# Two row vectors spread by VectorE, half rows interleaved on TensorE, and a new order of steps in a fused linear-attention and feed-forward kernel

## The chip, the cores and the metric

The kernel runs on one core of a Trainium2 chip. The metric is the time of one execution on the device in microseconds, the median of the runs. The engines are TensorE (PE; its weight loads are listed as PEld), VectorE (DVE), ScalarE (ACT), GpSimd (POOL) and SyncE (SP), which here only issues DMAs. Each engine works through its own list in order, and they meet at semaphores.

## The reference

```python
batch, n_heads, seq, head_dim = (4, 8, 768, 48)      # r, k, v; w and u are (n_heads, head_dim)
for t in range(S):
    cur = np.einsum('bhd,bhe->bhde', u[None] * kt, vt)
    y[:, :, t] = np.einsum('bhd,bhde->bhe', rt, state + cur)
    state = w[None, :, :, None] * state + np.einsum('bhd,bhe->bhde', kt, vt)
...
x = attn_out.transpose(0, 2, 1, 3).reshape(B * S, H * D)   # 3072 x 384
h = np.maximum(x @ w_in, 0.0)                              # w_in 384 x 2048
return h * h @ w_out                                       # w_out 2048 x 384
```

## The kernel before

The sequence is cut into chunks of 128 positions. A unit is one chunk of one batch with all eight heads, so there are 24 units, in the order of `UNITS`. Within a chunk the recurrence is written as products with a mask; between chunks a state per batch is carried along. Units 0 to 3 (two pairs, chunks 0 and 1 of batches 0 and 1) are loaded pair by pair: a partition of such a load holds two neighbouring positions, rows 0 to 63 belong to the first chunk and rows 64 to 127 to the second.

The whole program is one list of steps, `ORDER`, written out by hand or by a planner: name, unit or group, engine (P, D, A, G, S) and buffers or PSUM banks. A loop at the end issues the steps; each engine gets its own in the order of the list, and what stands between them on other engines is ordered only by the data, the buffers and the eight banks. The steps:

- `w`, `u` load the two vectors, `lw` takes the logarithm of w, `bw` and `bu` spread log w and u over 128 partitions by a product with a row of ones, `Wk` and `Wt` are the powers of w for k and r (Exp with a scale per partition; 0 and 1 for the pairs, 2 for the rest), `bc`, `WLcol` and `WLm` make the factor of a whole chunk.
- `lp`, `ld` load r, k, v (pairs, single units); `V` and `W` load quarters of the two weight matrices as bf16, from GpSimd's queue.
- `kh`, `rh` scale k and r into the tile rk; `vb` casts v. `P0`, `P1`, `du`, `dv` make the term with u. `TK`, `TR` with `KC`, `RC` transpose k and r of a pair; `T` with `Tc` does it for a unit on TensorE, `XB` by a DMA transpose.
- `A` (`Ap` for pairs) are the products k r, `Bm` (`Bp`) puts the mask on them, `Y` sums what goes to y, `U` is k v for the state, `S0`, `ts`, `S` carry the state.
- `xs` copies y out of PSUM, `X` and `xTc` transpose it on TensorE, `xX` by a DMA transpose.
- `F1` is a part of the first layer for a group of one or two units (`GROUPS`), `re` the maximum with 0, `sq` the square, `F2` a quarter of the second layer for a unit, `Fh` the same for half of the columns, `os` and `oh` copy out of PSUM, `out` and `outh` write to memory.
- `Z` are products of the identity with itself that nobody reads.

In `Y` and `U`, a unit of a pair uses only its 64 rows of the operands, and the two units of a pair are two separate steps. F1 has four parts per group of one unit and eight per group of two; a part fills one bank, which `re` must empty before the next user.

## Time and profile before

| | us |
|---|---|
| median of 3 runs (lowest, highest) | 172.89 (172.86, 173.21) |
| span of the profiled execution | 170.9 |
| TensorE busy | 163.7 |
| VectorE busy | 135.7 |
| ScalarE busy | 101.8 |
| GpSimd busy | 98.6 |
| granted TensorE clock, mean | 1.000 |

The profile covers one execution from its first to its last instruction; that is the span, and no other time is given for that execution. The time of a run has some microseconds around the span (172.89 against 170.9). Busy times of TensorE overlap, since a product's end is modelled and the next begins before it; the chain that ended last gives the pace of products better. In the groups of instructions a row names the line, the engine, the operation and its output and input tiles.

### The profile page before, as it was taken

How to read it: one execution, taken by the hardware profiler on the slowest of the kernel's cores; microseconds unless marked ns; L12 is line 12 of the kernel's file. 1: busy time of each engine (PE TensorE's matmuls, PEld its weight loads, DVE VectorE, ACT ScalarE, POOL GpSimd, SP SyncE). 2: the span in 40 equal slices, each digit the busy share in tenths (PEclk: the TensorE clock that was granted, in tenths of full speed). 3: DMA queues.
4: the chain of work that ended last, by engine and by line, in shares of the span. 5: the costliest groups of instructions: out<-in, count | busy, mean ns of one | idle time of the engine just before them, and what ended most of it. 6: DMA issues, size and time to landing. Idle time of an engine off the chain costs nothing.

```text
span 170.9 us, 4599 instructions
## 1 busy us (share of the span) xinstructions
PE 163.7 (96%) x1828; PEld 125.3 (73%) x1828; DVE 135.7 (79%) x255; ACT 101.8 (60%) x190; POOL 98.6 (58%) x120
## 2 busy tenths in 40 slices
...
GB/s 143 322 233 193 220 175 197 211 201 74 185 197 192 165 185 230 200 161 227 162 118 184 227 167 251 200 65 115 208 97 207 162 85 69 70 118 0 6 138 92
DMA packets 96297, 27.56 MB, mean 161 GB/s; under 512 B 90514, under 2 KB 96276, under 8 KB 96276
## 3 DMA queue, kind: packets, MB, share of 16 engines
...
q0 software_dynamic: 2688, 3.15, 10.7%
...
q14 instruction: 7, 0.06, 0.1%
...
## 4 chain that ended last, share of the span: by engine, by line
PE 76%; DMA 7%; POOL 7%; ACT 3%; SPq 2%; issue 2%; ACTq 0%; POOLq 0%
PE bank L532 29%; PE bank L504 29%; DMA ldk<-in_k_dram 3%; PE bank L410 3%; DMA ldr<-in_r_dram 2%; DMA out_dram<-os 2%; POOL rk L336 2%; POOL P L342 2%; PE bank L363 2%; PE bank L462 2%; SPq L320 2%; PE bank L451 2%; PE bank L546 2%; PE bank L488 1%; PE bank L449 1%
## 5 line engine op out<-in xcount | busy, mean ns | idle before, releaser
L504 PE MATMUL bank<-xT,W 128*128 128x256 bf16 (+1 forms) x672 | 70.0, 257 | 1.3 <-ACT hr L514 0.8
L532 PE MATMUL bank<-W,hq 128*128 128x384 bf16 x368 | 68.9, 326 | 0.0
L504 PEld LDWEIGHTS <-W 128*128 128x128 bf16 x672 | 57.1, 98 | 9.1 <-issue 1.5
L514 ACT ACTIVATE hr<-bank 128x512 bf16<-128x512 f32 x67 | 38.5, 594 | 35.4 <-PE bank L504 24.0
L532 PEld LDWEIGHTS <-hq 128*128 128x128 bf16 x368 | 33.7, 98 | 18.1
L521 ACT ACTIVATE hq<-hr 128x512 bf16<-128x512 bf16 x70 | 41.0, 626 | 3.4 <-DVE hr L516 2.8
L418 DVE TENSOR_TENSOR Bm<-bank,maskJT 128x512 bf16<-128x512 f32 x40 | 25.7, 681 | 2.7 <-PE bank L410 2.7
L516 DVE TENSOR_SCALAR hr<-bank 128x512 bf16<-128x512 f32 x29 | 19.8, 686 | 7.8 <-PE bank L504 5.3
L354 POOL TENSOR_TENSOR dv<-ldv,du 128x384 f32<-128x384 f32 (+1 forms) x18 | 15.9, 894 | 15.4 <-DVE du L349 10.5
L346 POOL TENSOR_TENSOR P<-P,ub 128x384 f32<-128x384 f32 x15 | 16.0, 1072 | 13.7 <-DVE P L342 13.3
L339 POOL TENSOR_TENSOR rk<-ldr,Wt 128x384 bf16<-128x384 f32 x15 | 16.1, 1081 | 0.0
L523 DVE TENSOR_TENSOR hq<-hr 128x512 bf16<-128x512 bf16 x26 | 12.8, 506 | 3.2 <-ACT hr L514 3.0
L483 POOL TENSOR_TENSOR S0W<-ts,WLm 128x384 bf16<-128x384 f32 x10 | 10.8, 1076 | 6.5 <-DVE ts L480 5.7
L342 POOL TENSOR_TENSOR P<-ldr,ldk 128x384 f32<-128x384 f32 x13 | 13.3, 1022 | 1.2 <-DMA ldk<-in_k_dram 1.1
L474 DVE TENSOR_TENSOR xs<-bank,dv 128x384 bf16<-128x384 f32 x20 | 11.1, 553 | 3.0 <-PE bank L451 1.1
L336 POOL TENSOR_TENSOR rk<-ldk,Wk 128x384 bf16<-128x384 f32 x12 | 12.6, 1054 | 0.7 <-DMA ldk<-in_k_dram 0.7
L349 DVE TENSOR_REDUCE du<-P 128x8 f32<-128x384 f32 x24 | 12.8, 542 | 0.0
L252 DVE COPY os<-bank 128x384 f32<-128x384 f32 x11 | 6.1, 551 | 6.6 <-PE bank L532 6.6
L250 ACT COPY os<-bank 128x384 f32<-128x384 f32 (+1 forms) x14 | 6.3, 460 | 7.2 <-DMA out_dram<-os 2.6
L480 DVE TENSOR_TENSOR ts<-bank,S0W 128x384 f32<-128x384 f32 x16 | 8.7, 549 | 1.2 <-POOL S0W L483 0.8
L451 PE MATMUL bank<-vb,Bm 128*128 128x48 bf16 x160 | 9.5, 183 | 0.0
L451 PEld LDWEIGHTS <-Bm 128*128 128x128 bf16 x160 | 8.2, 96 | 1.0
...
## 6 DMA issues: line engine op xcount, KB each, us to landing
...
```

What stands on the lines that cost most here:

```text
L336: e.tensor_mul(rk[slot[f"rk{i}"]][:, 1, :, 0:D], loaded("k", i), Do.factor("k", i % 2 if i < PAIRED else 2))
L339: e.tensor_mul(rk[slot[f"rk{i}"]][:, 0, :, 0:D], loaded("r", i), Do.factor("t", i % 2 if i < PAIRED else 2))
L342: e.tensor_mul(P0b[slot[f"P{i}"]], loaded("r", i), loaded("k", i))
L346: e.tensor_mul(t, t, bank("bu")[:, 0 : H * D].rearrange("p (h d) -> p h d", h=H) if i in EARLY_U else ub)
L354: e.tensor_mul(dv_of(i) if i < PAIRED else dvb[slot[f"dv{i}"]], loaded("v", i), t)
L418: e.tensor_mul(Bmb[slot[f"Bm{i}{h}"]], heads(bank(f"bA{i}{h}"), 128), mask_b)
L451: e.matmul(y[:, hc, D * h : D * (h + 1)], m[h][:, hc, :], vb[:, 2 * hc + h, :], start=(c == 0), stop=True, skip_group_check=True,)
L504: e.matmul(hp[:, fi, :], W1[f // 4][:, c, 256 * (f // 2 % 2) : 256 * (f // 2 % 2 + 1)].rearrange("p (m j) -> p j m", j=2)[:, f % 2, :], xt ...
L514: e.activation(hr, hp, AF.Relu)
L516: e.tensor_scalar_max(hr, hp, 0.0)
L521: e.activation(hq, hr, AF.Square)
L532: e.matmul(bank(f"bO{i}")[:, 0:d_model], hqb[slot[f"hq{g},{f // m}"]][:, at : at + L], W2[q][:, f % 4, :], start=(seen[i] == 1 and f % 4 = ...
```

## The change

- `w` and `u` are loaded into four partitions (0, 32, 64, 96) of cleared tiles, and VectorE's stream shuffle copies each of those rows to the 32 partitions of its quarter (`wsh`, `ush`). `lw` runs on 128 partitions, `Wk` and `Wt` read its output from SBUF. `bw`, `bu` and the copy `ub` go. `w` stays on ScalarE's queue, `u` moves to SyncE's.
- The clearing of the tiles rk beyond the first four and of WLm moves to GpSimd (`mR`, `mW`).
- For the pairs, `Y` becomes `YD` (both units of a pair in one step, with the products on rows 0 to 63 and 64 to 127 alternating) and `YI` (the part with the state); `U` becomes `UP`, alternating in the same way.
- The empty products, 8 + 2 + 7 in three places, become 28 at the start of TensorE's list.
- All steps have a new order and partly another engine. Steps by engine, before and after: sq on ScalarE 70 and 51, on VectorE 26 and 45; os on ScalarE 12 and 20, on VectorE 11 and 3; re on VectorE 29 and 25; kh on VectorE 12 and 7; rh on VectorE 9 and 13; T 3 and 5, XB 17 and 15; X 16 and 10, xX 8 and 14.

Removed code of functions is not repeated here; it stands above.

```diff
-EARLY_U = ()
 ORDER = """
-w:A mP.0:G mP.1:G lp.r.0:S/0 lp.k.0:S/0 tab:A lw:A Z.8:P/0 bw:P/0 lp.r.1:S/1 lp.v.0:S/0 mJ:G u:A lp.k.1:S/1 Wt.1:A/1
-lp.v.1:S/1 bc:P/2 P0.1:G/0 Wk.0:A/3 rh.1:D/0 ld.r.5:S/4 Wt.0:A/4 bu:P/5 kh.0:D/1 V.3:G WLcol:A P0.0:D/1 Wk.1:A/6
-rh.0:D/1 TR.0:P/7 ld.k.4:S/4 V.0:G rh.3:D/2 ub:A V.1:G rh.2:D/3 vb.0:A/0 vb.1:A/1 ld.r.4:S/5 kh.1:D/0 P1.0:G RC.0:A/0
-TR.1:P/2 kh.2:D/3 kh.3:D/2 TK.0:P/1 KC.0:A/1 V.2:G P1.1:D U.1:P/5 Z.2:P/4 TK.1:P/4 ld.k.5:S/5 du.0:D/0 dv.0:G RC.1:A/2
-du.1:D/1 dv.1:G Ap.0.1:P/7/3 Bp.0.1.1:D/0 vb.3:A/2 U.0:P/6 Ap.0.0:P/1/2 Bp.0.1.0:D/1 Bp.0.0.1:D/2 WLm:G KC.1:A/3
-Z.7:P/3 Ap.1.0:P/3/7 vb.2:A/3 U.3:P/2 Bp.0.0.0:D/3 P0.2:G/2 U.2:P/4 S0.0:D Y.0:P/1 ld.v.4:S/4 S0.2:D P1.2:G Y.1:P/6
-xs.0:A/0 ts.3:D/0 ts.1:D/1 X.0:P/4 Ap.1.1:P/1/2 xTc.0:D/0 du.2:D/2 xs.1:A/1 X.1:P/5 F1.0.3:P/4 xTc.1:A/1 P0.3:G/3
-P1.3:G Bp.1.0.1:D/4 F1.0.0:P/6 re.0.3:D/0 dv.2:G F1.1.3:P/5 Wt.2:A re.0.0:A/1 W.1:G Bp.1.1.1:D/5 du.3:D/3 ld.v.5:S/5
-Bp.1.0.0:D/6 Wk.2:A F1.1.0:P/4 F1.1.1:P/6 dv.3:G re.1.0:A/2 F1.0.1:P/0 rh.5:G/4 re.1.3:A/3 Bp.1.1.0:D/7 Y.3:P/4
-sq.1.3:A/0 re.0.1:A/4 W.2:G kh.4:D/5 re.1.1:A/5 sq.1.0:D/1 Y.2:P/5 ld.k.6:S/6 xs.3:D/2 W.3:G F1.0.2:P/0 xs.2:A/3
-rh.4:D/5 sq.0.0:A/2 X.3:P/6 W.0:G X.2:P/4 re.0.2:D/3 F1.1.2:P/5 xTc.3:A/0 sq.0.3:A/3 xTc.2:D/0 re.1.2:A/2 P0.4:D/4
-T.4:P/0 Tc.4:D/4 F1.2.4:P/6 F1.2.7:P/4 sq.1.2:D/4 F1.2.5:P/5 re.2.4:D/1 re.2.7:A/0 ld.r.6:S/6 sq.0.2:A/5 F1.2.1:P/0
...
+Z.28:P/0 lp.r.0:S/0 u:S nj:D w:A wsh:D tab:A ush:D lw:A bc:P/1 mW:G Wt.0:A/2 lp.k.0:S/0 rh.0:D/0 Wt.1:A/3 rh.1:D/1
+TR.0:P/4 Wt.2:A Wk.1:A/5 lp.k.1:S/1 mP.0:G Wk.0:A/6 mP.1:G P0.1:D/0 kh.1:D/1 P1.1:D WLcol:A RC.0:A/0 kh.0:D/0 TK.0:P/7
+KC.0:A/1 kh.3:D/3 kh.2:D/2 TK.1:P/0 KC.1:A/2 lp.r.1:S/1 rh.2:D/2 du.1:D/0 mJ:G P0.0:G/1 P1.0:G du.0:D/1 rh.3:D/3
+lp.v.0:S/0 vb.0:A/0 Ap.0.0:P/1/5 Bp.0.0.0:D/0 Ap.0.1:P/6/4 vb.1:A/1 ld.r.5:S/4 Bp.0.1.1:D/1 Bp.0.0.1:D/2 TR.1:P/2
+V.2:G Bp.0.1.0:D/3 UP.0:P/7/3 WLm:G S0.0:D RC.1:A/3 Ap.1.1:P/0/1 lp.v.1:S/1 Ap.1.0:P/4/5 V.3:G vb.2:A/2 dv.0:G dv.1:G
+YD.0:P/2/6 YI.1:P Bp.1.0.1:D/4 V.0:G vb.3:A/3 UP.1:P/7/5 Bp.1.0.0:D/5 ts.1:D/0 xs.0:A/0 X.0:P/2 xTc.0:D/0 Bp.1.1.0:D/6
+xs.1:A/1 X.1:P/4 F1.0.2:P/6 P0.3:G/2 P1.3:G du.3:D/2 xTc.1:A/1 P0.2:G/3 P1.2:G F1.1.2:P/3 Wk.2:A F1.1.3:P/2 F1.0.3:P/4
+Bp.1.1.1:D/7 du.2:D/3 dv.2:D re.1.3:A/0 sq.1.3:A/0 S0.2:D dv.3:G YD.1:P/0/1 xs.2:A/2 YI.3:P xs.3:A/3 F1.1.0:P/2
+re.0.3:A/1 mR:G F1.0.0:P/7 X.2:P/0 re.0.2:D/2 ld.k.5:S/4 X.3:P/6 V.1:G re.1.0:A/3 ts.3:D/1 re.1.2:A/4 kh.5:G/4
+rh.5:D/4 T.5:P/5 sq.1.2:A/1 ld.r.4:S/5 ld.k.4:S/5 kh.4:D/5 rh.4:G/5 T.4:P/1 Tc.4:A/4 xTc.3:D/0 xTc.2:D/0 F1.2.0:P/4
+P0.4:D/4 F1.2.1:P/2 re.2.1:A/5 F1.2.5:P/6 P0.5:G/0 re.0.0:A/0 Tc.5:D/5 ld.v.5:S/4 ld.r.6:S/6 P1.5:G P1.4:G W.1:G
+du.5:D/4 sq.2.1:A/2 re.2.0:A/4 A.5:P/3/0 sq.0.3:D/3 vb.5:A/4 A.4:P/5/1 sq.1.0:A/4 F1.2.7:P/2 rh.6:G/6 re.2.5:A/1
+ld.k.6:S/6 kh.6:G/6 du.4:D/0 dv.5:D F1.2.6:P/7 Bm.4.1:D/0 F1.2.3:P/1 re.2.3:A/5 F1.0.1:P/4 sq.0.2:A/5 F1.1.1:P/6
+re.1.1:A/3 ld.v.4:S/5 sq.1.1:A/6 dv.4:G ld.k.10:S/7 U.5:P/1 Bm.4.0:D/1 Bm.5.0:D/2 Bm.5.1:D/3 Y.5:P/5 re.0.1:A/2
+ld.r.7:S/7 vb.4:D/5 Y.4:P/3 T.6:P/0 F1.2.2:P/6 xs.5:D/4 ld.k.9:S/1 X.5:P/5 xs.4:D/0 ld.k.7:S/0 ld.v.7:S/6 S0.5:D
+xTc.5:D/1 Tc.6:D/6 sq.2.3:D/7 re.2.6:D/3 S.3:G X.4:P/3 F1.2.4:P/4 xTc.4:A/1 U.4:P/1 S0.4:D ld.v.6:S/7 sq.2.5:D/8
...
+sq.3.4:A/18 ld.k.12:S/4 F1.3.7:P/6 re.3.7:A/4 F2.3.1:P/7 Y.6:P/0 Y.7:P/6 F2.2.3:P/1 F2.3.3:P/7 F2.2.0:P/1 os.2:A/0
+dv.7:G xs.7:D/1 ld.r.13:S/4 X.7:P/6 xTc.7:A/2 rh.9:D/2 xs.6:D/2 X.6:P/0 xTc.6:A/2 ts.6:D/0 ld.v.9:S/0 sq.3.5:D/19
+re.3.0:A/3 P0.9:D/3 XB.9:S/2 F2.0.0:P/3 sq.3.1:D/20 F2.5.2:P/5 F1.4.5:P/1 S.6:D rh.8:D/3 F2.1.3:P/2 os.3:A/1 rh.10:G/0
+F1.4.3:P/6 F1.4.7:P/0 re.4.3:A/0 P0.8:D/0 re.4.5:D/2 F1.4.2:P/4 ld.k.11:S/5 F1.4.0:P/7 A.9:P/1/6 sq.3.3:A/21 P1.9:D
+P1.8:G sq.4.3:D/22 re.4.2:D/1 sq.4.5:A/23 re.4.0:A/0 du.8:D/3 re.4.7:A/5 F2.1.0:P/2 os.1:A/2 sq.3.0:A/24 F1.4.6:P/4
+re.4.6:A/2 sq.4.6:A/25 vb.9:D/0 Bm.9.0:D/2 F1.4.4:P/7 F2.0.3:P/3 re.4.4:A/3 rh.13:D/4 Bm.9.1:D/3 kh.8:G/3 P0.10:G/4
+ld.r.11:S/5 P0.11:D/2 ld.k.13:S/0 P1.11:D ld.v.10:S/1 P1.10:D sq.3.7:A/26 os.0:A/3 F2.4.1:P/0 T.10:P/1 Tc.10:A/0
+sq.4.4:D/27 U.9:P/2 F2.5.1:P/5 F2.4.2:P/0 kh.13:G/4 kh.11:D/5 Y.9:P/6 P0.13:G/1 sq.4.7:D/9 A.10:P/4/7 du.9:D/4
+XB.8:S/3 dv.9:D xs.9:D/3 A.8:P/3/1 Bm.8.1:D/0 Bm.8.0:D/1 ld.v.8:S/3 du.10:D/0 ld.v.13:S/2 rh.12:D/1 vb.10:A/1
+sq.4.2:A/6 F2.4.3:P/0 rh.11:G/5 ld.v.11:S/4 XB.11:S/5 F1.4.1:P/6 out.2:S re.4.1:A/2 F2.4.0:P/0 vb.8:G/2 Y.8:P/1 dv.8:G
+xs.8:D/4 ts.9:D/0 F2.6.3:P/3 du.11:D/2 F2.6.2:P/3 X.8:P/6 A.11:P/1/2 F2.6.1:P/3 xX.9:S/0 xTc.8:A/0 kh.12:G/1
+F1.5.7:P/6 F2.5.3:P/5 sq.4.0:D/5 Bm.10.0:D/4 Bm.10.1:D/5 re.5.7:A/4 sq.5.7:A/1 U.8:P/4 P1.13:D Bm.11.1:D/6 ld.r.15:S/6
+os.4:D/0 ld.r.20:S/7 S.7:G Bm.11.0:D/7 F1.5.3:P/7 vb.11:D/3 P0.15:G/0 F1.5.1:P/6 re.5.1:A/3 ld.k.14:S/6 P0.12:D/3
+P1.12:D F1.5.6:P/2 re.5.6:A/5 Y.11:P/0 sq.4.1:D/8 XB.12:S/4 out.1:S F1.5.0:P/1 re.5.0:A/1 dv.11:G Y.10:P/6 dv.10:G
+F1.5.2:P/2 re.5.2:A/0 xs.10:D/0 du.12:D/1 F2.5.0:P/5 xs.11:D/1 F2.7.0:P/1 re.5.3:D/4 ld.r.14:S/0 rh.14:G/6 os.5:A/2
+F1.5.5:P/6 S.9:D ts.8:D/1 out.0:S X.11:P/2 xTc.11:A/1 out.4:S F1.5.4:P/0 kh.14:G/6 re.5.4:A/2 XB.13:S/6 S.8:D
+ld.r.16:S/1 kh.15:G/2 A.13:P/5/7 A.12:P/4/2 Bm.12.0:D/2 F2.6.0:P/3 sq.5.0:A/15 os.6:A/3 F2.7.2:P/1 rh.15:D/2 xX.10:S/1
+U.11:P/0 sq.5.4:A/7 ld.k.16:S/1 F1.6.6:P/4 F2.7.1:P/1 ld.k.17:S/2 sq.5.1:A/14 ld.v.12:S/5 vb.12:G/4 Bm.12.1:D/3
+sq.5.6:D/12 F2.9.3:P/3 Bm.13.1:D/0 F1.6.2:P/2 du.13:D/4 F1.6.0:P/7 re.6.6:A/1 F2.9.0:P/3 re.5.5:D/2 sq.5.5:D/17
+U.10:P/4 rh.16:D/3 ts.11:D/0 U.12:P/6 Bm.13.0:D/1 ld.v.15:S/7 vb.13:A/5 P1.15:G re.6.0:A/5 sq.5.3:D/2 P0.14:G/4
+P1.14:D du.14:D/3 dv.12:G kh.16:G/3 sq.5.2:A/16 re.6.2:A/3 F2.7.3:P/1 os.7:A/0 du.15:D/0 dv.15:G out.5:S F1.6.1:P/0
+F1.6.4:P/7 dv.13:D ld.r.17:S/3 ld.r.18:S/4 XB.14:S/1 S.11:G F2.9.2:P/3 F2.8.3:P/5 XB.15:S/2 re.6.1:D/2 sq.6.1:D/11
+Y.13:P/2 xs.13:D/2 ld.k.19:S/7 ld.v.17:S/6 Y.12:P/1 xs.12:D/3 ts.10:D/1 F2.8.0:P/5 vb.15:G/6 ld.v.14:S/3 re.6.4:A/0
+ts.12:D/0 sq.6.4:D/0 kh.17:G/5 F1.6.5:P/7 F2.9.1:P/3 re.6.5:A/4 sq.6.5:A/4 sq.6.6:A/3 vb.17:A/7 S.12:D A.15:P/0/2
+Bm.15.0:D/6 rh.18:G/0 sq.6.2:A/13 XB.16:S/3 A.14:P/1/4 Bm.14.0:D/7 xX.13:S/2 U.15:P/6 F2.8.2:P/5 F2.8.1:P/5 F1.6.7:P/7
+re.6.7:A/2 rh.17:G/5 Bm.15.1:D/4 vb.14:G/0 S.10:G F1.6.3:P/0 dv.14:G xX.12:S/2 Bm.14.1:D/5 P0.16:D/2 U.14:P/1
+ts.14:D/0 re.6.3:A/0 kh.19:G/1 ld.v.19:S/0 Y.15:P/2 xs.15:D/4 sq.6.3:A/21 Y.14:P/4 XB.17:S/5 U.13:P/7 ts.13:D/1
+sq.6.7:D/18 xs.14:D/1 S.13:G P0.17:D/3 ld.k.18:S/0 ld.r.19:S/5 F1.7.0:P/0 re.7.0:A/4 F1.7.6:P/1 P1.16:G F1.7.4:P/2
+F1.7.2:P/7 ld.v.16:S/1 ts.15:D/1 A.16:P/0/4 Bm.16.0:D/0 os.9:A/2 re.7.6:A/1 out.7:A re.7.4:A/3 sq.7.4:A/19 A.17:P/3/1
+Bm.17.1:D/1 rh.20:G/2 Bm.17.0:D/2 F2.10.2:P/6 re.7.2:A/0 sq.7.0:A/10 rh.19:D/1 os.8:A/0 out.8:A F2.11.2:P/2 F1.7.5:P/0
...
+F2.22.0:P/7 outh.23.1:S os.22:A/3 out.22:S F2.20.0:P/5 os.20:D/2 out.20:A F2.18.1:P/3 os.18:A/0 F2.21.0:P/6 out.3:S
+F2.21.2:P/6 F2.19.0:P/0 out.18:A os.21:D/3 Fh.23.0.0:P/1 out.21:A F2.19.3:P/0 Fh.23.1.0:P/1 Fh.23.2.0:P/1 os.19:A/2
+out.19:S Fh.23.3.0:P/1 oh.23.0:A/1 outh.23.0:S
 """
...
+    half = H * D // 2
+    nc.vector.memset(wsrc[:, 0:half], 0.0)
+    nc.gpsimd.memset(wsrc[:, half:], 0.0)
+    nc.gpsimd.memset(usrc, 0.0)
+    nc.vector.memset(LW[0:1, :, D:DP], 0.0)
     nc.vector.memset(ones, 1.0)
+    for t in rk[:PAIRED]:
+        nc.vector.memset(t[:, :, :, D:DP], 0.0)
...
+        def spread(e, t, row):
+            e.dma_start(
+                out=t.rearrange("(a q) n -> a q n", a=4)[:, 0, :],
+                in_=bass.AP(tensor=row.tensor, offset=row.offset, ap=[[0, 4], [1, H * D]]),
+            )
         def w(e):
+            Do.spread(e, wsrc, w)
         def u(e):
+            Do.spread(e, usrc, u)
+        def wsh(e):
+            e.stream_shuffle(wspr, wsrc, [0] * 32)
+        def ush(e):
+            e.stream_shuffle(ub.rearrange("p a b -> p (a b)"), usrc, [0] * 32)
         def tab(e):
             e.preload_act_table_set("natural_log_exp_and_others")
         def lw(e):
+            e.activation(LW[:, :, 0:D], wspr.rearrange("p (h d) -> p h d", h=H), AF.Ln)
+        def nj(e):
+            e.tensor_scalar(njcol, tcol, -1.0, -1.0, op0=ALU.mult, op1=ALU.add)
+        def mR(e):
+            for t in rk[PAIRED:]:
+                e.memset(t[:, :, :, D:DP], 0.0)
+        def mW(e):
+            e.memset(WLm, 0.0)
...
+        def spreading(e, o, scale):
+            e.activation(o, LW[:, :, 0:D], AF.Exp, scale=scale)
...
+        def half(x):
+            return slice(64 * x, 64 * x + 64)
+        def YD(e, q):
+            y = [heads(bank(f"bY{2 * q + x}"), 2 * D) for x in range(2)]
+            for a in range(2):
+                for x in range(2):
+                    e.matmul(
+                        y[x][Do.half(a)], identity[Do.half(x), Do.half(x)],
+                        dv_of(2 * q + a)[Do.half(x)].rearrange("p (a e) d -> p a (e d)", e=2),
+                        start=True, stop=False, skip_group_check=True,
+                    )
+            for hc in range(HP):
+                for h in range(2):
+                    for a in range(2):
+                        for x in range(2):
+                            e.matmul(
+                                y[x][:, hc, D * h : D * (h + 1)],
+                                Bmb[slot[f"Bm{q}{a}{h}"]][Do.half(x), hc, :],
+                                vbb[slot[f"vb{2 * q + a}"]][Do.half(x), 2 * hc + h, :],
+                                start=False, stop=True, skip_group_check=True,
+                            )
+        def YI(e, i):
+            y = heads(bank(f"bY{i}"), 2 * D)
+            rT = rkTb[slot[f"rT{i // 2}"]].rearrange("p x y -> p (x y)").rearrange("p (h c t) -> p h c t", h=HP, c=2)
+            for hc in range(HP):
+                e.matmul(
+                    y[:, hc, :], rT[:, hc, i % 2, :], S0W[UNITS[i][0]][:, hc, :],
+                    start=False, stop=True, skip_group_check=True,
+                )
...
+        def UP(e, q):
+            o = [heads(bank(f"bU{2 * q + x}"), 2 * D) for x in range(2)]
+            for hc in range(HP):
+                for a in range(2):
+                    for x in range(2):
+                        e.matmul(
+                            o[x][:, hc, :],
+                            pair(rk[slot[f"rk{2 * q + a}"]], 1, hc)[Do.half(x)],
+                            vbb[slot[f"vb{2 * q + a}"]][Do.half(x), 2 * hc : 2 * hc + 2, :].rearrange("p a b -> p (a b)"),
+                            start=(a == 0), stop=(a == 1), skip_group_check=True,
+                        )
```

191 lines of the change are left out of this document (56 added, 135 removed).

## The prediction

> **What bounds the kernel now.** I read the page's busy times first, then the busy time by stretches, then who waited for whom, then the chain that ended last and the timeline of the start.
>
> ```profile
> PE 163.7 (96%) x1828; PEld 125.3 (73%) x1828; DVE 135.7 (79%) x255; ACT 101.8 (60%) x190; POOL 98.6 (58%) x120
> ```
> ```profile
> 17.66:69.00 51.34, 51.34 (x604) 39.37 (x602) 46.41 (x87) 34.15 (x63) 30.41 (x34) 1.00 0.98 187
> 101.30:167.60 66.30, 66.30 (x695) 51.04 (x694) 47.00 (x85) 38.05 (x73) 26.26 (x28) 1.00 0.54 119
> 167.60:170.90 3.30, 0.00 (x1) 0.00 (x0) 0.00 (x0) 0.32 (x1) 0.00 (x0) 1.00 0.19 64
> ```
> ```profile
> PE bank L504 <- ACT hr L514: 0.8, 1, 0.8
> PE bank L504 <- ACT os L250: 0.5, 1, 0.5
> ```
>
> Columns of the second view are the stretch, its length, then busy time of TensorE (PE), of its weight loads, of VectorE (DVE), of ScalarE (ACT) and GpSimd (POOL). From the first product of the first layer (17.66) to the last product (167.60) TensorE stands still only 1.3 us, in two waits near 98 and 101. So the span is a start of 17.66, 149.9 of nearly unbroken products, and a tail of 3.30 in which the last rows go out. The products of the reference are the same after the change. What can move is when the first layer starts, how full its first microseconds are, the stalls, and the tail.
>
> The units of work come from the chain (start, length, line, count):
>
> ```profile
> 17.82 4.02 PE bank L504 x72
> 25.46 0.46 PE bank L397 x8
> 25.92 4.59 PE bank L504 x42
> 30.95 0.65 PE bank L532 x4
> 32.26 0.33 PE bank L410 x8
> 38.73 0.17 PE bank L488 x3
> 38.90 0.17 PE bank L462 x4
> 53.29 0.04 PE bank L449
> 53.66 0.65 PE bank L532 x4
> 62.14 0.55 PE bank L410 x16
> ```
>
> A step F1 is 0.67 for a single unit (12 products, 4.02/6) and 0.66 for a pair (4.59/7); F2 0.65; A 0.33 alone and 0.55 for two neighbours; X 0.17; U 0.17; Y 0.37 (53.29 to 53.66); T 0.46.
>
> **Part 1, the start.** Now:
>
> ```profile
> 0.81 0.53 ACTq L256 DMA_DIRECT2D wrow<-in_w_dram  x1
> 1.37 1.28 ACT L262 ACT_TABLE_LOAD   x1 [1.37 <-PEq L619]
> 2.66 0.52 ACT L265 ACTIVATE lrow<-wrow 1x384 f32<-1x384 f32 x1
> 2.95 0.38 DVE L233 MEMSET WLm<- 128x384 f32 x1
> 4.92 0.56 ACT L297 ACTIVATE bank<-bank,tcol 128x384 f32<-128x384 f32 x1 [1.73 <-PE bank L268]
> 5.51 0.55 DVE L339 TENSOR_TENSOR rk<-ldr,bank 128x384 bf16<-128x384 f32 x1 [2.18 <-ACT bank L297]
> 6.92 1.47 DVE L339 TENSOR_TENSOR rk<-ldr,bank 128x384 bf16<-128x384 f32 x3
> 8.28 0.93 ACT L250 CAST vb<-ldv 128x384 bf16<-128x384 f32 x2
> 9.11 1.01 ACT L250 COPY rkT<-bank 128x1024 bf16<-128x1024 bf16 x1
> 10.72 1.01 DVE L349 TENSOR_REDUCE du<-P 128x8 f32<-128x384 f32 x2
> 12.15 2.48 DVE L391 TENSOR_TENSOR Bm<-bank,maskP 128x512 bf16<-128x512 f32 x4 [0.43 <-PE bank L383]
> 17.18 0.36 DVE L252 COPY xT<-bank 128x384 bf16<-128x384 bf16 x1 [0.43 <-PE bank L488]
> 17.66 4.18 PE L504 MATMUL bank<-xT,W 128*128 128x128 bf16 x72
> ```
>
> VectorE decides it: from its first rh (5.51) to the end of xTc.0 (17.54) are 12.0 us with little idle time. The path to 5.51 is w's load, Ln, the product bw, Exp.
>
> The change takes bw out and puts a shuffle in. w's DMA now waits for the clearing of wsrc, half on VectorE and half on GpSimd. Half of the 0.38 clearing is 0.2, and GpSimd comes to its own half after its constants, so the DMA starts at about 1.2 instead of 0.81. Ln ran 1.85 after that DMA began, and only the table load held it (1.37 + 1.28 = 2.65), so w lands by 3.05 at the latest. The shuffle has no row; nearest are one pass over 384 columns (0.55, the rh row), and the table load's 1.28 as an upper end that nothing here is likely to reach; I take 0.5. Then Ln on 128 rows as long as an Exp (0.56), Exp 0.56: 3.05 + 0.5 + 0.56 + 0.56 = 4.7, with hand-overs 4.9. So rh.0 starts 0.6 earlier (bounds 0.3 later, 1.0 earlier). [...]
>
> On VectorE's new list from rh.0 to xTc.0 stand four rh, four kh, P0.1, P1.1, two du, S0.0 and ts.1, that is 14 at 0.50 (1.47/3, 1.01/2), six Bp at 0.62 (2.48/4) and 0.36: 11.1. With 0.2 of waiting for Wk.1 (ScalarE does Wt.2 first) xTc.0 ends at 16.2 and F1 starts at 16.35, 1.3 earlier. ScalarE's copies before (RC.0, KC.0, KC.1, two vb, RC.1; 1.01 for each of the four, 0.47 for a vb) run from about 7.4, behind three Wt, two Wk and WLcol, with a wait of 0.3 for TK.0, to 12.7; the two Ap.1 then end near 13.6, some 0.5 before VectorE asks for them, so a later ScalarE eats the gain beyond that.
>
> Next, four F1 (2.7) end at 19.05. YD.1 needs dv.2, which on VectorE comes two Bp, two du and a dv after xTc.0: 16.2 + 2.8 = 19.0. YD.1 and YI.3 are the old Y.2 and Y.3 with their halves side by side; neighbours A fall from 0.66 to 0.55 that way, and I take 1.1 (0.9 to 1.8). Two F1, X.2, X.3, T.5, T.4: 2.6. F1.2.0 then starts at 22.8. The old kernel starts this group at 25.92, having done two F1 more and one T less (0.9). Equal progress is 23.7: a gain of 2.2, 1.3 of it from the start. What can hold it is k of unit 4, now fourth among the single loads instead of second:
>
> ```profile
> 8.03 1.18 SPq L320 DMA_DIRECT2D ldk<-in_k_dram  x1
> DMA to landing us min/median/max: 13.3/13.3/13.3
> ```
>
> It landed at 21.3; kh.4 now wants it at about 21.3 again, ahead of xTc.3 and xTc.2 on the same engine. One quarter of W1 less is in flight by then. I take off 0.2: **-2.0** (bounds -0.5 and -2.4).
>
> **Part 2, the products behind it.** Two more T (+0.92), six X fewer (-1.02): **-0.1**. The six go to DMA transposes and two come back from them; Y.9, the first of them, has 5.5 us of products before its F1, so it is hidden unless SyncE's queue (XB.8, XB.11 and v loads ahead of it) is late. Pairs of A: eight before, eight after. The two old stalls (1.3) hang on output rows still being written; with 20 instead of 12 os copies on ScalarE and another out order I take both as gone: **-1.3** (0 to -1.3).
>
> **Part 3, VectorE in the middle.** The change moves 19 sq to VectorE (26 to 45), eight os and five kh away, four rh, two vb to it. From xs.7 to ts.15 it now has 89 instructions; TensorE between Y.7 and F2.10.2, which need the first and wait for the last, has 31 F2, 28 F1, 10 A, 8 Y, 8 U, 4 X, 1 T = 20.2 + 18.4 + 3.0 + 3.0 + 1.4 + 0.7 + 0.5 = 47.0. The nearest rows are the old middle, and a square:
>
> ```profile
> 40.00:90.00 50.00, 46.18 (x83) 1.00 0.95 176
> ```
> ```profile
> 61.00 0.41 DVE L523 TENSOR_TENSOR hq<-hr 128x512 bf16<-128x512 bf16 x1
> 59.46 0.69 DVE L516 TENSOR_SCALAR hr<-bank 128x512 bf16<-128x512 f32 x1
> 76.69 1.82 DVE L342 TENSOR_TENSOR P<-ldr,ldk 128x384 f32<-128x384 f32 x2
> ```
>
> 46.18/83 is 0.556 each. The new stretch has 13 squares where the old had five, so 81 x 0.556 + 8 x 0.41 = 48.3, 1.3 over TensorE's 47.0. Undisturbed (16 Bm at 0.62, 13 sq at 0.41, 5 re at 0.69, 55 at 0.49) it is 45.7: no stall. With all 89 at 0.556 and the idle share of the old stretch (3.8 of 50) it is 53.1: a stall of 6.1. VectorE had 3.8 of slack in those 50; now it has none, and what it waits for counts. I take 1.3 + 0.7: **+2.0** (0 to 6.1).
>
> **Part 4, the tail.** The last steps are again half rows; out.19, a whole block, is issued one Fh ahead of the last: **+0.2** (0 to 0.6).
>
> Sum: -2.0 - 0.1 - 1.3 + 2.0 + 0.2 = **-1.2** on a span of 170.9. The median of the runs, 172.89, is 2.0 above it, and I take that as fixed: **171.7 us**.
>
> **The rivals.**
> *VectorE becomes the bound (slower).* The 76.69 row speaks for it: 0.9 per P0 where a quiet one takes 0.55, with GpSimd busy. Against it: squares are short, and much of the work is ahead of need. At 6.1 of stall the time is 171.7 + 4.1 = 175.8; it is slower than now once the stretch stalls over 3.2 us, so over 0.564 per instruction with no wait at all, or 0.556 with 0.7 us more waits.
> *The stretch costs nothing.* Then 169.7.
> *Weights or loads come late.* GpSimd issues the W1 quarters behind P0.0, P1.0 and the dv:
>
> ```profile
> 5.44 1.00 POOL L342 TENSOR_TENSOR P<-ldr,ldk 128x384 f32<-128x384 f32 x1 [1.08 <-DMA ldk<-in_k_dram]
> 11.35 1.61 POOL L354 TENSOR_TENSOR dv<-ldv,du 128x384 bf16<-128x384 f32 x2 [0.72 <-DVE du L349]
> 6.38 2.48 POOL L330 DMA_DIRECT2D W<-in_moe_w_in_dram  x3
> DMA to landing us min/median/max: 6.2/9.2/11.0
> ```
>
> V.2 now goes out after P0.0 and P1.0 (5.5 + 2.0 = 7.5) and has until 16.35. V.0 goes out after the two dv, which wait for du.0 (near 10.7; + 1.6 = 12.3), and has until F1.1.0 at 20.2, which is 7.9. At the 9.2 median it is 1.3 late; then 173.0. In its favour: the quickest landed in 6.2, and fewer quarters are in flight.
> *The first layer starts at half clock.*
>
> ```profile
> 7.80 2.74 PE L363 MATMUL bank<-identity,rk 128*128 128x128 bf16 x24
> ```
>
> These 24 run at 0.11 each, until 10.5, where F1's of the same width take 0.056. The granted clock is 1.00 throughout, so it shows only in such rows. 28 empty products at 0.11 are 3.1 us, about as long as that slow time, so I expect the switch before TR.0. But TensorE is then only half busy until 16, with no filling products. If F1 pays 2.7 us of that, it loses half, 1.4: 173.1. [...]
> *The halves do not run side by side.* Then YD.1 costs 1.8: 172.4.
>
> **How the numbers follow.** Forecast 0.37, free stretch 0.17, halves not overlapping 0.06, late weights 0.11, half clock 0.07, VectorE bound 0.22. A measurement of this kernel can tell 0.2% (0.35 us): below 172.54 is faster, above 173.24 slower. Forecast, free stretch and most of the halves' case give faster 0.58; late weights and clock lie mostly between, 0.15; VectorE's case and the rest 0.27. The range goes from the free stretch to near VectorE's case: 169.7 to 175.2; the forecast's own is 170.6 to 172.5.
>
> **What would show it.** Right: first rh near 4.9, first F1 near 16.4, group 2 near 22.8; TensorE waiting for VectorE by about 2 us between the Y.7 and F2.10.2 steps and nearly nowhere else; VectorE over 95% busy there. Wrong: F1 at 17.5 or later, products of W1 waiting for DMA, F1 of 128 columns at 0.11, or VectorE's stretch over 50 us.

## The result and the profile after

The changed kernel takes 192.42 us (median of 4 runs, 191.62 to 194.07) where the kernel before, run beside it, took 172.88 (4 runs, 172.60 to 173.21). The ratio is 1.1141, 95% interval 1.1088 to 1.1193: 11% slower. The prediction was 171.7, with 169.7 to 175.2 as its range. The profiled execution spans 190.9, which is 20.0 more than before. Some executions of several kernels here took a few per cent longer than the others of the same kernel: a time below is the median of all, a ratio is taken without them, and of `e12_gpsimd_memsets` only the profiled run, 176.22, counts so, while its five others took 180.0 to 181.7.

The page of the profile after, busy times, and the clock in its 40 slices:

```profile
PE 169.7 (89%) x1821; PEld 127.6 (67%) x1821; DVE 154.2 (81%) x266; ACT 98.5 (52%) x182; POOL 97.1 (51%) x119
...
PEclk9999999799999996699999999999999999999999
```

VectorE is busy 18.5 us longer with 11 instructions more, GpSimd no longer than before. The clock has two dips, in the eighth slice (33 to 38 us) and near 73 to 80. The same profile by stretches (length, then busy time of TensorE, weight loads, VectorE, ScalarE, GpSimd, then clock, DMA share, GB/s):

```profile
19.03:40.00 20.97, 15.21 (x231) 13.37 (x231) 20.94 (x24) 11.52 (x22) 18.24 (x23) 0.92 1.07 193
...
64.00:120.00 56.00, 50.90 (x522) 37.22 (x520) 52.75 (x88) 31.03 (x59) 36.13 (x37) 0.94 0.84 165
120.00:157.00 37.00, 34.13 (x350) 24.98 (x348) 34.60 (x58) 14.77 (x29) 20.48 (x21) 1.00 0.60 124
...
187.82:190.90 3.08, 0.00 (x1) 0.00 (x0) 0.00 (x0) 0.32 (x1) 0.00 (x0) 1.00 0.26 96
55.37:112.37 57.00, 52.16 (x538) 37.87 (x535) 53.49 (x90) 29.67 (x56) 34.15 (x34) 0.94 0.81 157
```

In the two stretches left out, 40 to 64 and 157 to 187.82, TensorE is busy all the time. It stands for 5.76 us in the first row (20.97 - 15.21), 5.10 in the second and 2.87 in the third, together 13.7, where before it stood for 1.3 in all. In the first row VectorE works without a gap (20.94 of 20.97) and finishes only 24 instructions. The 20.0 us are then: first layer later by 1.4 (19.03 against 17.66), stalls 12.4 (13.7 - 1.3), busy time of the products 6.4 (155.1 against 148.6), tail -0.2.

The busy time of the products grows at the two dips. Timeline of TensorE at the two longest stalls and at four products of F2 on either side of the second, then the stretches over each dip, whose clock is the third number from the end:

```profile
35.21 3.71 PE L536 MATMUL bank<-xT,W 128*128 128x256 bf16 x30 [3.43 <-DVE Bm L433]
69.88 0.82 PE L564 MATMUL bank<-W,hq 128*128 128x384 bf16 x4
74.13 1.44 PE L536 MATMUL bank<-xT,W 128*128 128x256 bf16 x6 [3.43 <-DVE xs L506]
75.36 1.49 PE L564 MATMUL bank<-W,hq 128*128 128x384 bf16 x4
```
```profile
35.50:39.00 3.50, 3.50 (x33) 3.30 (x32) 3.50 (x4) 1.12 (x2) 3.50 (x5) 0.51 1.12 192
73.00:80.00 7.00, 5.87 (x33) 3.40 (x32) 5.50 (x12) 0.60 (x1) 0.85 (x1) 0.51 0.78 159
```

Four products of F2 take 0.82 at full clock (69.88) and 1.49 in the dip (75.36). The clock is 0.51 over these 3.5 us and 7.0 us. About half of the products' time there is lost: 3.50 x 0.49 + 5.87 x 0.49 = 4.6 of the 6.4. The rest of the 6.4 is waits too short for the view to part them from work; that is an inference.

What TensorE waited for is seen on VectorE. Its timeline around the first stall, and GpSimd's at the same time:

```profile
23.13 2.68 DVE L354 TENSOR_TENSOR rk<-ldr,Wt 128x384 bf16<-128x384 f32 x1
25.73 1.34 DVE L351 TENSOR_TENSOR rk<-ldk,Wk 128x384 bf16<-128x384 f32 x1
27.53 0.54 DVE L357 TENSOR_TENSOR P<-ldr,ldk 128x384 f32<-128x384 f32 x1
29.85 4.70 DVE L369 TENSOR_TENSOR dv<-ldv,du 128x384 f32<-128x384 f32 x1
34.48 2.47 DVE L433 TENSOR_TENSOR Bm<-bank,maskJT 128x512 bf16<-128x512 f32 x4
36.87 2.87 DVE L253 CAST vb<-ldv 128x384 bf16<-128x384 f32 x1
```
```profile
29.10 0.76 POOL L348 DMA_DIRECT2D W<-in_moe_w_out_dram  x1
29.88 1.01 POOL L354 TENSOR_TENSOR rk<-ldr,Wt 128x384 bf16<-128x384 f32 x1
30.84 1.00 POOL L351 TENSOR_TENSOR rk<-ldk,Wk 128x384 bf16<-128x384 f32 x1
31.80 0.83 POOL L369 TENSOR_TENSOR dv<-ldv,du 128x384 f32<-128x384 f32 x1
32.59 0.99 POOL L515 TENSOR_TENSOR S0W<-ts,WLm 128x384 bf16<-128x384 f32 x1
33.52 1.48 POOL L348 DMA_DIRECT2D W<-in_moe_w_out_dram  x2
```

The step dv.5 takes 4.70 where undisturbed rows of its kind take 0.55. It begins a moment before rh.6 on GpSimd and ends behind four GpSimd steps, rh.6, kh.6, dv.4, S.3. The four Bm that TensorE wants at 35.21 stand behind it. At 27.53, while GpSimd waits for its operand, VectorE does a P0 in 0.54. The products with one operand in a bank (Bm, 2.47 for four) keep their usual length. The groups of two kinds of VectorE's steps with all operands in SBUF (hq, dv), before and then after, and of Bm after, show how general that is (the number ahead of the second bar is the mean ns of one):

```profile
L523 DVE TENSOR_TENSOR hq<-hr 128x512 bf16<-128x512 bf16 x26 | 12.8, 506 | 3.2 <-ACT hr L514 3.0
...
L354 DVE TENSOR_TENSOR dv<-ldv,du 128x384 f32<-128x384 f32 x6 | 3.9, 649 | 0.0
```
```profile
L433 DVE TENSOR_TENSOR Bm<-bank,maskJT 128x512 bf16<-128x512 f32 x40 | 26.2, 680 | 0.7 <-PE bank L425 0.7
L555 DVE TENSOR_TENSOR hq<-hr 128x512 bf16<-128x512 bf16 x45 | 24.9, 565 | 6.5 <-ACT hr L546 6.1
...
L369 DVE TENSOR_TENSOR dv<-ldv,du 128x384 f32<-128x384 f32 x7 | 9.1, 1300 | 0.1
```

Below, a "hold" is what such a step takes beyond 0.41 us (a square), 0.55 (a product of 384 columns) or 0.35 (a cast). Summed over all groups of that kind it is 9.9 us in 73 steps before and 27.7 in 98 after.

The theory: VectorE's steps whose operands are all in SBUF wait while GpSimd reads SBUF; the new order and split put more of them beside unbroken runs of GpSimd, VectorE becomes what TensorE waits for, and stalls of 3.4 us bring the half clock on top. The rivals: a new part of the code is slow; the order itself is late, whatever VectorE's steps take; loads and DMA transposes come late in SyncE's queue; the 45 squares are too many.

### The profile page after: what moved, and what is told of

It reads as the page before. It is cut to its first block, busy times and chain, and to the rows that moved or that the text cites. A ratio compares the mean times of both kernels' runs of the same rounds, so it can differ in the third digit from the quotient of the medians.

```text
span 190.9 us, 4592 instructions
## 1 busy us (share of the span) xinstructions
PE 169.7 (89%) x1821; PEld 127.6 (67%) x1821; DVE 154.2 (81%) x266; ACT 98.5 (52%) x182; POOL 97.1 (51%) x119
## 4 chain that ended last, share of the span: by engine, by line
PE 42%; DVE 27%; POOL 9%; issue 8%; DMA 7%; SPq 4%; ACT 2%; DVEq 0%; POOLq 0%; ACTq 0%
PE bank L564 18%; PE bank L536 15%; DVE Bm L433 4%; DVE rk L354 3%; DVE hq L555 3%; DVE du L364 3%; POOL rk L351 2%; SPq L335 2%; DVE vb L253 2%; POOL S0W L515 2%; DMA ldr<-in_r_dram 2%; DMA xT<-xs 2%; DVE rk L351 2%; DVE hr L548 2%; DMA ldk<-in_k_dram 2%
## 5 line engine op out<-in xcount | busy, mean ns | idle before, releaser
L536 PE MATMUL bank<-xT,W 128*128 128x256 bf16 (+1 forms) x672 | 74.1, 263 | 9.3 <-DVE xs L506 4.1
L546 ACT ACTIVATE hr<-bank 128x512 bf16<-128x512 f32 x71 | 41.4, 597 | 51.3 <-PE bank L536 44.5
L553 ACT ACTIVATE hq<-hr 128x512 bf16<-128x512 bf16 x51 | 31.4, 628 | 4.6 <-DVE hr L548 3.0
L555 DVE TENSOR_TENSOR hq<-hr 128x512 bf16<-128x512 bf16 x45 | 24.9, 565 | 6.5 <-ACT hr L546 6.1
L548 DVE TENSOR_SCALAR hr<-bank 128x512 bf16<-128x512 f32 x25 | 17.0, 684 | 5.6 <-PE bank L536 5.1
L351 POOL TENSOR_TENSOR rk<-ldk,Wk 128x384 bf16<-128x384 f32 x17 | 19.1, 1132 | 0.0
L361 POOL TENSOR_TENSOR P<-P,ub 128x384 f32<-128x384 f32 x13 | 14.3, 1103 | 7.6 <-DVE P L357 7.3
L251 ACT COPY os<-bank 128x384 f32<-128x384 f32 (+1 forms) x21 | 9.9, 469 | 14.8 <-PE bank L564 10.4
L354 POOL TENSOR_TENSOR rk<-ldr,Wt 128x384 bf16<-128x384 f32 x11 | 12.3, 1121 | 2.1 <-DMA ldr<-in_r_dram 2.1
L369 DVE TENSOR_TENSOR dv<-ldv,du 128x384 f32<-128x384 f32 (+1 forms) x8 | 9.7, 1208 | 0.1
```

The lines of the kernel that those rows point to most:

```text
L351: e.tensor_mul(rk[slot[f"rk{i}"]][:, 1, :, 0:D], loaded("k", i), Do.factor("k", i % 2 if i < PAIRED else 2))
L354: e.tensor_mul(rk[slot[f"rk{i}"]][:, 0, :, 0:D], loaded("r", i), Do.factor("t", i % 2 if i < PAIRED else 2))
L369: e.tensor_mul(dv_of(i) if i < PAIRED else dvb[slot[f"dv{i}"]], loaded("v", i), t)
L536: e.matmul(hp[:, fi, :], W1[f // 4][:, c, 256 * (f // 2 % 2) : 256 * (f // 2 % 2 + 1)].rearrange("p (m j) -> p j m", j=2)[:, f % 2, :], xt ...
L546: e.activation(hr, hp, AF.Relu)
L548: e.tensor_scalar_max(hr, hp, 0.0)
```

## The experiments

All times are medians; the ratio is to the kernel before on the same chip.

### The parts without the order

`e1_old_order` has every new part (spreading by shuffle, halves, 28 empty products first) and the order and split of before.

```diff
-w:A ... lw:A Z.8:P/0 bw:P/0 ... u:A ... bu:P/5 ... ub:A ... U.1:P/5 Z.2:P/4 ... Z.7:P/3 ... Y.0:P/1 ... Y.1:P/6
+Z.28:P/0 w:A u:S wsh:D ush:D mW:D mR:D ... UP.0:P/6/5 ... UP.1:P/4/2 ... YD.0:P/1/6 ... YI.1:P
```

> All new parts of the code (shuffles for w and u, the 28 empty products first, YD/YI/UP for the pairs) in the order of the kernel before, which keeps every later step where and on which engine it was. If the order is at fault (and with it what stands beside what), the time comes back to the kernel before within the parts' own cost: the first rh was 0.6 us later in the changed kernel (6.11 against 5.51) and the pairs' Y cost 1.66 - 0.98 = 0.7 less, so 172 to 174 us. If the parts are at fault, it stays above 180 us.

175.33 us, ratio 1.0074 (0.9970 to 1.0179), hold 10.0. So the parts alone do not make 11%. Its first layer starts late, though, and the clock is down there. TensorE's timeline, and the clock in the 40 slices of 4.34 us:

```profile
19.35 5.47 PE L536 MATMUL bank<-xT,W 128*128 128x128 bf16 x72
```
```profile
PEclk9997599999999999999999999999999999999999
```

The old kernel started it at 17.66 and did the 72 products in 4.18. The fourth and fifth slice are the trace's half clock, 15.22 to 22.05: the first 2.7 us of the first layer ran in it. So the prediction's rival "the first layer starts at half clock" did come true in this kernel, and its price of 1.4 us fits (5.47 - 4.18 = 1.3).

`e11_old_fill` is that kernel with the empty products in their three old places.

```diff
-Z.28:P/0
+Z.8:P/0 ... Z.2:P/4 ... Z.7:P/3
```

> The kernel with all new parts in the old order (first F1 at 19.35, against 17.66 before), with the old three fillings of 8, 2 and 7 empty products among the transposes instead of the 28 ahead of them. If the empty products' new place leaves TensorE at half clock to 16 us (its products for A and Y ran at half pace there), the half pace ends near 11 us as in the kernel before and F1 starts near 18.0: 1.2 us less than with the 28, 172 to 173 us where the kernel before takes 172.9. If the shuffles alone delay the start (the first rh at 6.3 against 5.5), F1 stays at 19 or later and the time is the same as with the 28.

173.25, ratio 1.0013 (0.9981 to 1.0045), first layer at 18.51 and at full clock. By this pair the place of the empty products costs 0.8 us at the start (19.35 - 18.51), and the spreading by shuffle some 0.7 (18.51 against 17.81 for the halves alone, next). Each of these starts is one execution, and the changed kernel's own start moved by 1.25 between two (19.03 and 17.78, below), so the two shares are not shown. What repeats is the first rh: it begins at 6.11 to 6.29 in the four traces `after`, `c_after`, `e1_old_order` and `e11_old_fill`, and at 5.50 to 5.51 in `before` and in the two kernels that follow here.

`e6_halves` is the kernel before with the halves side by side and nothing else.

```diff
-U.1:P/5 U.0:P/6 U.3:P/2 U.2:P/4 Y.0:P/1 Y.1:P/6 ... Y.3:P/4 Y.2:P/5
+UP.0:P/6/5 UP.1:P/4/2 YD.0:P/1/6 YI.1:P ... YD.1:P/5/4 YI.3:P
```

> The kernel before with one part of the change alone: YD, YI and UP for the two pairs, in the place of Y and U, nothing else moved. The two Y of the second pair took 1.66 us, a YD and its YI took 0.98 in the changed kernel; of the first pair the same, but it lies ahead of the first layer, where VectorE sets the pace. If TensorE is the bound there as the profile says: 0.7 us faster (0.4 to 1.3), a ratio of 0.996 (0.993 to 0.998). If the halves' gain is hidden by VectorE in both places: within 0.2 us.

171.84 (8 runs), ratio 0.9910 (0.9877 to 0.9943): the halves alone are worth 0.9%, a little more than expected, and this kernel beats both. Its timeline of TensorE has the step that was in dispute:

```profile
21.92 0.36 PE L427 MATMUL bank<-dv,identity 64*64 64x384 bf16 x4
...
22.72 0.34 PE L447 MATMUL bank<-S0W,rkT 128*128 128x96 bf16 x4
```

From 21.92 to the next step at 22.97 are 1.05 us for Y of two units, which took 1.84 in the kernel before (21.77 to 23.61).

`e10_halves_out` adds one move, to see whether the last short stall, on an output row, can go too.

```diff
-out.4:A
+out.4:S
```

> The kernel before with YD, YI and UP (ratio 0.991 alone), and the issue of out.4 moved from ScalarE's queue to SyncE's at the same place. In that run ScalarE stood 2.3 us until 96.5 us at this issue (it waited for another transfer), and TensorE then 0.63 + 0.16 us for ScalarE. If that wait goes and none takes its place: 0.8 us less, a ratio to the kernel before of 0.987 (0.985 to 0.989). If SyncE's queue now stands there and its loads and transposes come later: 0.991 or above.

171.67, ratio 0.9913 (0.9880 to 0.9946): no gain over `e6_halves`. TensorE waited 0.86 us for ScalarE's hr and 1.03 for its os.

### How long one hold lasts

`e2_sliver` does rh.5, kh.4, dv.5 and vb.4 on one of eight heads.

```diff
-            e.tensor_mul(dv_of(i) if i < PAIRED else dvb[slot[f"dv{i}"]], loaded("v", i), t)
+            n = 1 if i == 5 else H
+            e.tensor_mul(o[:, 0:n], loaded("v", i)[:, 0:n], t[:, 0:n])
```

> The changed kernel, in which four VectorE steps that lasted very long (rh.5 2.68, kh.4 1.34, dv.5 4.70, vb.4 2.87 us) work on one head of eight; the other seven heads of these four keep zeros. If such an instruction is held until GpSimd's run of work pauses, its length does not depend on its size: rows of 2.0 to 2.6, 0.9 to 1.3, 4.2 to 4.7 and 2.4 to 2.9 us remain, and the time stays within 1.5 us of 192.4. If GpSimd only slows VectorE's traffic byte by byte, they shrink to 0.2 to 0.6 us, the 3.43 us stall near 35 us goes, and the time falls by 5 us or more, to 187 or less.

186.84, ratio 1.0715 (1.0555 to 1.0875). Its timeline of VectorE:

```profile
21.66 2.33 DVE L362 TENSOR_TENSOR rk<-ldr,Wt 128x48 bf16<-128x48 f32 x1
27.19 4.35 DVE L379 TENSOR_TENSOR dv<-ldv,du 128x48 f32<-128x48 f32 x1
33.85 0.18 DVE L253 CAST vb<-ldv 128x48 bf16<-128x48 f32 x1
```

An eighth of the work takes 4.35 us instead of 4.70, and 2.33 instead of 2.68. So the length of these two is a wait and not the step's own work. The other two were not held this time: kh.4 took 0.20, and the cast fell into a pause of GpSimd. The time missed its range. Stalls of 3.36 and 3.42 remain, but only the second is followed by half clock, for 3.4 us, where the changed kernel has 10.2 us of it; that saves about 2.9, and the first layer, which started at 17.56, another 1.5. Of the 5.3 that the span is shorter (185.6) most comes from these two and not from the smaller steps.

`e4_moved` takes the longest holds away by engine: dv.5 to GpSimd, vb.4 to ScalarE, kh.6 behind dv.4.

```diff
-kh.6:G/6 du.4:D/0 dv.5:D ... dv.4:G ... vb.4:D/5
+du.4:D/0 dv.5:G ... vb.4:A/5 ... dv.4:G kh.6:G/6
```

> The changed kernel with two VectorE steps moved: dv.5 to GpSimd (ahead of dv.4, with kh.6 behind both) and vb.4 to ScalarE. The result is the same. If the hold of dv.5 and vb.4 made the stalls of 3.43 and 0.43 us near 35 and 39 us and the half clock behind the first of them (1.5 us), all of that goes: 187 us (186 to 188.5). If VectorE is late there for another reason, or the time is lost again later, 190 us or more.

186.56, ratio 1.0726 (1.0619 to 1.0834). `c_after` is the changed kernel unedited, run again in another group:

> The changed kernel once more, unaltered, beside the other kernels: the same stalls of 3.4 us near 35 and 74 us, and a time near 192 us. What it can add is whether the first F1 starts at 19.0 again, or at 17.5 as in two of the kernels derived from it whose steps up to there are the same or nearly so.

189.21, ratio 1.0918 (1.0881 to 1.0955), hold 24.0. It is 2% nearer to the kernel before than in the first comparison; its first layer started at 17.78 instead of 19.03, and both stalls of 3.43 were there, the second with 3.4 us of half clock behind it instead of 6.8. In `e4_moved` the first of them is gone (TensorE works from 27.73 to 39.79 without a gap) and the second is not, as TensorE's timeline has it:

```profile
69.36 0.81 PE L536 MATMUL bank<-xT,W 128*128 128x256 bf16 x6 [3.49 <-DVE xs L506]
```

So the first stall was made by the held steps that were moved. (The start of that trace is late again, 18.96, as in `after`.)

`e15_weights_early` issues all weight loads but one early, since the longest holds begin just behind such an issue on GpSimd.

```diff
-V.0:G ... V.1:G ... W.1:G ... W.2:G ... W.0:G
+V.0:G V.1:G W.1:G W.2:G W.0:G
```

> The changed kernel with four of GpSimd's weight loads (V.1, W.1, W.2, W.0) issued right after V.0, some 4 to 15 us earlier, and nothing else moved. In every trace so far the VectorE steps that were held through several GpSimd steps (2.3 to 4.7 us) stand within 4.5 us behind a DMA issue by GpSimd; elsewhere a hold ends with the GpSimd step that it met (at most 1.35 to 1.4 us). If the issue makes the difference, rh.5 (2.68), dv.5 (4.70) and vb.4 (2.87) fall to 1.4 or less here though GpSimd's run beside them is the same, the 3.43 us stall near 35 us falls below 1, and the time is about 3 to 5 us less, 184 to 188 us. If it is the unbroken run itself, dv.5 still takes over 3 us and the time stays within 1.5 us of 189 to 192.

192.00, ratio 1.1075 (1.0958 to 1.1192): the time does not move. The lengths do. rh.5 falls from 2.68 to 1.23, dv.5 is 0.56 and vb.4 0.71; but at the one issue that stayed in the middle there is a new long one. VectorE's timeline and GpSimd's:

```profile
40.91 2.71 DVE L555 TENSOR_TENSOR hq<-hr 128x512 bf16<-128x512 bf16 x1
```
```profile
40.59 0.76 POOL L348 DMA_DIRECT2D W<-in_moe_w_out_dram  x1
41.37 1.01 POOL L515 TENSOR_TENSOR S0W<-ts,WLm 128x384 bf16<-128x384 f32 x1
42.33 0.99 POOL L351 TENSOR_TENSOR rk<-ldk,Wk 128x384 bf16<-128x384 f32 x1
```

A square of 0.41 is held through two GpSimd steps. That GpSimd itself waited longer in this run is a second reason why dv.5 was short there, so the part of the issue is not shown by this run alone.

`e7_more_gpsimd` leaves the order alone: the kernel before, with 14 products on GpSimd that nobody reads, in three of its idle times.

```diff
+        def more(e, n):
+            for _ in range(n):
+                e.tensor_mul(idle, ub, Wk)
+ ... vb.4:G/4 more.5:G ... kh.6:G/0 more.4:G ... vb.9:G/1 more.5:G
```

> The kernel before, nothing moved, with 14 products of 384 columns more on GpSimd (about 1.0 us each, of constants into a buffer that nobody reads), in three of its idle times: five from 26.3 us, four from 40.8, five from 57.5, all done before its next step is due. If GpSimd at work holds VectorE, VectorE's steps with all operands in SBUF get longer there, it has 1.2 us to spare in 10, and TensorE comes to wait: 2 to 8 us slower, 175 to 181 us. If only the order of the steps matters, idle time of GpSimd is free to use: within 0.5 us of the kernel before.

179.48, ratio 1.0355 (1.0291 to 1.0419), hold 16.9 instead of 9.9. GpSimd's timeline, and VectorE's:

```profile
42.79 5.00 POOL L577 TENSOR_TENSOR idle<-ub,Wk 128x384 f32<-128x384 f32 x4
```
```profile
44.30 1.35 DVE L342 TENSOR_TENSOR rk<-ldr,Wt 128x384 bf16<-128x384 f32 x1
45.58 1.35 DVE L339 TENSOR_TENSOR rk<-ldk,Wk 128x384 bf16<-128x384 f32 x1
46.85 1.35 DVE L349 TENSOR_TENSOR P<-P,ub 128x384 f32<-128x384 f32 x1
```

Here a hold is one GpSimd step long: the two engines take turns, and both are slowed (1.25 for an idle product). With the order of before, 14 more steps on GpSimd cost 3.5%. In the first of the three places they also delayed dv.4 by some 2.8 us, so not all of it is the hold, and this run does not part what GpSimd reads from its being busy.

### All of GpSimd's reading

`e3_gpsimd_sliver` is the changed kernel with GpSimd's steps on one head; it leaves out the rest of their work.

```diff
+            n = 1 if e is nc.gpsimd and t in full else H
-            e.tensor_mul(P0b[slot[f"P{i}"]], loaded("r", i), loaded("k", i))
+            e.tensor_mul(P0b[slot[f"P{i}"]][:, 0:n], loaded("r", i)[:, 0:n], loaded("k", i)[:, 0:n])
```

> The changed kernel with its order, in which GpSimd's elementwise steps (kh, rh, P0, P1, dv, vb, S) work on one head of eight (S: one pair of four) wherever the buffer has been filled before; the rest keeps older values. If VectorE is held by GpSimd's work, the VectorE steps with all operands in SBUF go back to 0.55 (squares 0.41) behind the first units, TensorE's stalls behind 40 us (8 us) and the half clock near 75 us (2.6 us) go, and the time is 178 to 183 us. If the order alone feeds the engines too late (loads, waits, VectorE's longer list), it stays at 188 us or more.

178.15, ratio 1.0211 (1.0041 to 1.0380). Most of the loss is gone. But GpSimd is also early now, so `e12_gpsimd_memsets` fills the time that it saved with clearings of a tile, which write and do not read.

```diff
+            if n == 1:
+                nc.gpsimd.memset(fill, 0.0)
+                nc.gpsimd.memset(fill[:, 0:6], 0.0)
```

> As the run with GpSimd's elementwise steps on one head of eight (178 us), but each of those shortened steps is preceded by two clearings of a buffer that nobody reads (0.42 and about 0.33 us), which bring GpSimd's time back to about 1.0 us a step: it is as busy and as late as in the changed kernel, but reads SBUF for 0.3 us of each step alone. If VectorE is held by GpSimd's reading, its rows with all operands in SBUF stay short and the time is 177 to 181 us. If it was GpSimd's own lateness that cost the time, 186 us or more. [...]

Its page and the groups of VectorE:

```profile
PE 161.4 (93%) x1821; PEld 123.1 (71%) x1821; DVE 131.0 (75%) x266; ACT 98.0 (56%) x182; POOL 96.3 (55%) x263
```
```profile
L580 DVE TENSOR_TENSOR hq<-hr 128x512 bf16<-128x512 bf16 x45 | 18.8, 426 | 8.1 <-ACT hr L571 7.9
L389 DVE TENSOR_TENSOR dv<-ldv,du 128x384 f32<-128x384 f32 x7 | 3.9, 551 | 0.1
```

The run took 176.22, its span 174.5; as a single run it has no interval. All six runs lie between 176.2 and 181.7, those of the unedited changed kernel between 189.1 and 194.1, and the others of the six have no trace. GpSimd is as busy as in the changed kernel (96.3 against 97.1), with the same order and split, and the hold falls from 27.7 to 3.8. VectorE's busy time falls by 23.2 and the span by 16.4. This is the strongest evidence: the larger part of the 20.0 comes from what GpSimd reads, not from its being late and not from the order as such. How large a part is less sure: 16.4 by this run, some 11 by the five longer ones. The Bm rows, with one input in a bank, take 0.682 here, 0.680 in the changed kernel and 0.681 before: no hold shows in them in any of the three.

### Single repairs

Three kernels on top of `e4_moved` tested what else was late: `e5_squares` gives 19 squares back to ScalarE, `e8_loads` issues ten loads ahead of the DMA transposes XB.9 and XB.11 in SyncE's queue, `e9_loads_squares` does both.

```diff
-sq.2.3:D/7 ... sq.3.2:D/13 ... sq.2.2:D/14 ... sq.6.0:D/24 ...
+sq.2.3:A/7 ... sq.3.2:A/13 ... sq.2.2:A/14 ... sq.6.0:A/24 ...
```
```diff
-XB.9:S/2 ... ld.k.11:S/5 ... ld.r.11:S/5 ... ld.k.13:S/0 ... ld.v.10:S/1 ... ld.v.8:S/3
+ld.k.11:S/5 ld.r.11:S/5 ld.k.13:S/0 ld.v.10:S/1 ld.v.8:S/3 ... XB.9:S/2
```

> The changed kernel with dv.5 on GpSimd and vb.4 on ScalarE as before (that alone gave 186.6 us), and with the 19 squares of groups 2 to 8 that the change took from ScalarE to VectorE given back to ScalarE (45 squares on VectorE become 26). The result is the same. If VectorE, held and loaded, is what TensorE waits for in the rest too, then the 3.5 us stall near 69 us and the half clock behind it (6 us together) and some 4 us of the smaller waits to 157 us go: 177 us (175 to 180). If late loads and GpSimd's own waits set the pace, less than 3 us go: 183.5 us or more.

185.18, ratio 1.0722 (1.0659 to 1.0785).

> The changed kernel with dv.5 and vb.4 moved (186.6 us alone), and with ten loads of r, k and v moved ahead on SyncE's queue: seven ahead of the DMA transpose XB.9, three ahead of XB.11. Their buffers are free by then. The result is the same. In the changed kernel SyncE's queue stood 9.5 us behind XB.9 (which waits for rh.9 on VectorE), the DMA engines moved nearly nothing from 47 to 57 us, and GpSimd later stood still 7.5 and 6.3 us for loads. If the blocked queue is a second cause, those waits go and the time is 180 to 184 us. If only what VectorE meets from GpSimd counts, loads that come earlier change little: 185.5 to 187.5.

187.24, ratio 1.0731 (1.0660 to 1.0801).

> The same with the 19 squares given back to ScalarE as well, which without the earlier loads brought only 1.4 us (185.2), because TensorE then waited for DMA transposes (2.3 and 1.1 us) in place of VectorE. If late loads and late transposes are what took its place: 178 us (175.5 to 181). If not: 184 or more.

185.38, ratio 1.0664 (1.0598 to 1.0730). In all three the hoped-for gain did not come: beside 1.0726 for `e4_moved` none gives back as much as 1%. With the squares away the stall at 69.36 fell to 1.32, and a wait of 2.3 for a DMA transpose took its place; with the loads moved it was 1.7 for ScalarE and 2.3 for a transpose; with both, 2.5 and 1.7 for VectorE. So neither the number of squares nor the late loads, alone or together, carries much of the rest.

### Order and split apart

`e13_after_old_engines` has the new order with 181 steps on the engines of before; `e14_before_new_engines` has the order of before with the new engines, the same edit the other way round. The first:

```diff
-P0.1:D/0 ... P0.0:G/1 ... kh.5:G/4 ... rh.5:D/4 ... dv.2:D
+P0.1:G/0 ... P0.0:D/1 ... kh.5:D/4 ... rh.5:G/4 ... dv.2:G
```

> The order of the changed kernel, with every elementwise step that both kernels have (181 differ) on the engine that it has in the kernel before. If the new split between VectorE, GpSimd and ScalarE makes the time: 180 us or less. If the new order does, whatever the split: 186 us or more.

221.38, ratio 1.2790 (1.2695 to 1.2884), hold 12.6.

> The other way round: the kernel before with its own order and its own parts, its 181 steps on the engines that the changed kernel gives them. If the split makes the time: 183 us or more. If the order does: 178 us or less. If it is the two not fitting each other, both this and the run before are slow.

198.83, ratio 1.1534 (1.1444 to 1.1623), hold 21.6; its first layer, too, ran in part at half clock (72 products in 6.11). Each is worse than both together. The order and the split were fitted to one another, so neither can be named as the guilty half. The first also shows that a schedule can be much later with little hold (TensorE stands still for 34 us behind its first F1): the hold explains the changed kernel, not every bad order.

## Why the prediction was wrong

**The term that failed is Part 3, VectorE in the middle.** It put 81 of 89 instructions at 0.556 and eight squares at 0.41 against 47.0 us of products (its own terms add up to 47.2) and took a stall of 2.0. The stretch from Y.7 (55.37) to F2.10.2 (112.37) is the last row of the stretches above: 57.0 us, 10.0 over the products' 47.0. VectorE spent 53.49 in it on 90 records, 0.594 each; the text had named 0.564 as the point from which it decides, and over 50 us as a sign of being wrong. It was busy 94% of the stretch, near the 95% that would have shown the step right. Of the 10.0, 4.8 is standing still (57.00 - 52.16) and 2.9 the half clock in it; 2.3 stays without a name. The long stall in it, 3.43 up to 74.13, hangs on xs.9, which copies y out of the bank that F1 writes next. No step ahead of xs.9 is held through several of GpSimd's: from 61.05 to 73.42 eleven steps with all operands in SBUF take 4.5 us more than quiet ones, these two the most (VectorE's timeline):

```profile
69.55 1.21 DVE L555 TENSOR_TENSOR hq<-hr 128x512 bf16<-128x512 bf16 x1
70.69 1.34 DVE L351 TENSOR_TENSOR rk<-ldk,Wk 128x384 bf16<-128x384 f32 x1
```

Two things were mis-sized. The duration was taken as a mean of the old order, though its source, GpSimd beside it, is what a new order changes. And a stall was taken to cost its own length only. (The list of moved steps also left out two P1, two dv and one S that came to VectorE, which have all operands in SBUF.)

**The same mechanism outside the middle had no term at all.** Between 19.03 and 40.00, 5.76 us stand still and 1.7 are lost to the clock; behind 120, another 2.87. The prediction compared VectorE's work with TensorE's over 50 us. The long holds hit single steps that TensorE needs at once: 4.70 ahead of Bm.4 and 2.87 ahead of Y.4. Reckoned as the prediction does it, at equal progress, group 2 starts 2.65 late (27.67 + 0.9 - 25.92); with 10.0 in the middle and the tail 0.2 shorter, some 7.5 of the 20.0 is left to stretches that had no term for VectorE.

**The rival "VectorE becomes the bound" had the mechanism right** (it named the P0 row of 0.9 beside a busy GpSimd), at a chance of 0.22 and 175.8 us. Its price came from a mean with some holds in it, and its upper end, 6.1, bounded the middle alone.

**Part 1, the start: -1.3 forecast, +1.4 measured** at the first F1, and at group 2, where the term of -2.0 was taken, it missed by more. Timeline of VectorE and TensorE after:

```profile
4.33 0.58 DVE L269 STREAM_SHUFFLE wspr<-wsrc 128x384 f32<-128x384 f32 x1
6.11 1.05 DVE L354 TENSOR_TENSOR rk<-ldr,bank 128x384 bf16<-128x384 f32 x2 [0.72 <-ACT bank L306]
```
```profile
2.54 3.17 PE L595 MATMUL bank<-identity 128*128 128x512 bf16 x7 [2.54 <-POOL identity masks.py:199]
16.07 0.82 PE L451 MATMUL bank<-vb,Bm 64*128 64x48 bf16 x32
...
19.03 2.84 PE L536 MATMUL bank<-xT,W 128*128 128x128 bf16 x48 [0.31 <-DVE xT L253]
21.80 0.36 PE L442 MATMUL bank<-dv,identity 64*64 64x384 bf16 x4
22.09 0.57 PE L451 MATMUL bank<-vb,Bm 64*128 64x48 bf16 x32
22.60 0.34 PE L462 MATMUL bank<-S0W,rkT 128*128 128x96 bf16 x4
...
27.67 2.14 PE L536 MATMUL bank<-xT,W 128*128 128x256 bf16 x18
```

The shuffle took 0.58 where 0.5 was forecast, 0.08 of the loss. But w landed at 4.33 where 3.05 was called the latest: "the latest" was read off the old load into one partition, which landed at most 1.85 after its issue, and the new one, into four, landed 3.1 after its issue at 1.23; why is not shown. So rh.0 began at 6.11 instead of 4.9. The empty products, 3.2 us long, did not bring the full pace: 32 products of YD.0 still took 0.82 at 16.07 where the same of YD.1 took 0.57 at 22.09. The trace's record of the granted clock begins, at full, only at 18.48 (in the kernel before at 10.72), and a view gives 1.00 for the time ahead of it; so "the granted clock is 1.00 throughout" was read where nothing was recorded. F1 began at 19.03 instead of 16.35. Group 2 started at 27.67, not 22.8: the term of 0.2 taken off for kh.4 was in truth rh.5's 2.68 and kh.4's 1.34.

**What held.** YD.1 with YI.3 took 0.98 (21.80 to 22.78) against 1.1 forecast; the halves do run side by side. F1 of 128 columns ran at 0.059 each, so the rival of half clock in the first layer did not happen in this execution (it did in `e1_old_order`). No product of W1 waited for its weights. The two old stalls are gone but for 0.3 us on hr, and the tail is 0.2 shorter where 0.2 more was forecast.

**How much the theory carries.** With the holds gone (`e12_gpsimd_memsets`) the span is 174.5, 16.4 of the 20.0 back in the one run with a trace; 3.6 remain. That figure takes in the half clock, which followed the stalls, and the earlier start of that trace (17.80). What stays open is why moving single steps gave back so little: `e4_moved` removed one of the two longest stalls and the ratio came down to 1.0726 (from 1.0918 in `c_after`), and each further repair handed the wait to a DMA transpose, to ScalarE or to VectorE again.
